# A planned S4D and SwiGLU kernel on one core: modulation columns as four tasks, the spectrum input loaded in four parts, one filling product for eight, and the plan's tasks dealt anew

## The chip, the core and the metric

The kernel runs on one core of a Trainium2 chip. The metric is the device time of one execution in microseconds (us). Engines are called as in the profile: PE is TensorE (PEld its weight loads), DVE is VectorE, ACT is ScalarE, POOL is GpSimd, SP is SyncE, which here issues nearly all DMAs. A change of the time by 0.2% (1.9 us) is about what a measurement of this kernel can tell from none.

## What is computed

```python
sa, ca, ga, sb, cb, gb = split(silu(c) @ w_mod)          # six rows of 640
h = layernorm(x) * (1 + ca) + sa                          # x: 2048 tokens x 640
K = 2 * real(sum_n C[d,n] * exp(A[d,n] * dt[d] * l))      # 640 kernels of 2048 taps, n < 128
y = irfft(rfft(h.T, 4096) * rfft(K, 4096))[:, :2048].T + h * D_skip
x = x + ga * y
h = layernorm(x) * (1 + cb) + sb
x = x + gb * ((silu(h @ w1) * (h @ w3)) @ w2)             # 640 -> 1728 -> 640
```

## The kernel before

**Two stages.** The first stage (0 to about 373 us) makes the long convolution. Channels go in five blocks of 128 (b = 0 to 4). For each block the kernel normalises the input (tasks h), makes the 128 kernels (tasks t, g), brings both into a spectrum (hh and k, then w), multiplies them and transforms back (w, z), and stores the result in DRAM (zd). The second stage (from about 382 us to the end) reads it back, adds it to x, and does the gated network as matrix products, four groups of 512 tokens: `ln2`, `ffn`, `pair_up`, `pair_down`.

**What sets the order in the first stage.** The work is cut into 1492 tasks (`Plan.add`, L177). A task names its engine or a choice of engines and the tasks it comes after. `ORDER` (L34) is the finished plan: the numbers of the tasks in the order in which `Plan.run` (L183) emits them, with a letter (a, d, p for ACT, DVE, POOL) where the engine was a choice. `InOrder` (L136) chains each engine's instructions in just that order, and semaphores do the rest. An engine whose next instruction waits does nothing else. `took`, `rank`, `take`, `give` and `port` are what the planner was told of durations, urgency and buffers; they have no effect on the chip. As every instruction of this stage is recorded through the helper at L146, most groups of the profile have that line; the tile names tell them apart.

**Modulation columns.** The second half of w_mod (sb, cb, gb) comes in five loads c0 to c4, with five products mc0 to mc4 into one PSUM tile pm (`mod_row`, L287). One task, `cols` (added at L1799, put down for ACT at 0.9 us), then calls `mod_cols` (L1247): POOL clears a corner of a tile mc, ACT copies pm into it twice, PE turns it with four products into the PSUM tile pv, and DVE writes the three columns with three small operations. All of that stands at one place of the order on each of the four engines. The last block pool (`inv`, L1125) and all products of the w tasks come after `cols`.

**A block's spectrum input.** h{b}.i.l loads a quarter of the block's x, h{b}.i.n, x and a normalise it, h{b}.i.o stores it in DRAM (hs), and h{b}.f (L1429) calls `h_fetch` (L356): four DMAs of 256 KB, one after the other, that bring the block back turned, as the tile xb. The eight products hh{b}.0 to 7 (L1448 and on) need all four.

**Behind TensorE.** A DMA that is issued while `behind` is set on SP's wrapper waits for the last PE instruction that was emitted before it (L142 to L153). `run` uses it for early loads of the second stage (fx, fw, iz: `paced`, L1145).

**The end of the first stage.** z4.3 is the last inverse product; its two halves are stored by SP, and `inverse_load` at L1208 (its DMA line is L568) reads the last block's columns for the first tokens: four DMAs from SP and four from ACT. `awake` (L1825) issues matmuls whose result nobody reads: eight (L1209), then come the inverse products (`inverse`, L1210, its lines L583 and L588), then three more (L1211), then `ln2`. The token loads of `load_x2` are held until the inverse's last product (`self.hold`), and the weights of the third tile until the reads of L1208. The first two weight tiles are loaded in the first stage and split there: fa0, fa1 (high parts, ACT), fs0, fs1 (low parts, POOL; L1173).

**Block 4 on POOL.** In the last block two of the eight spectrum products, w4.2 and w4.5, are multiplied on POOL (x0, x1, c) from a copy that ACT makes (kk); the others on DVE.

Of the kernel before, what the change touches and what calls it, by code (L numbers as in the profile page):

```python
# [10 lines left out]
F32 = mybir.dt.float32  # L11
# [7 lines left out]
P = 128  # L19
# [15 lines left out]
1 2 8 7 12 78 80 3 79 86 81 41 14 19 82 20 42 84 21 15 83 43 85 16 150p 44 17 4 22 151 18 23 28 61 45 59 30 120 31 46 121 24  # L35
10 29 25 39 153 35 26 13 62 154 60 155 47 72 74 70 76 66 89 27 48 5 93 87 91 98 49 36 100 33 95 50 94 34 51 32 88 37 52 38
152p 40 92 156d 53 96 157 90 9 158 6 54 102 159 167 104 55 170 99 11 171 168 97 56 103 183 176 172 57 105 178 173 169 58 187
184 111 177 107 185 67 192 101 122 186 68 188 174 193 160 194 189 64 179 175 123 190 180 109 161 163d 65 181 191 199 113 310
114 115 110 196 182 112 295 117 200 332 203 118 108 201 208 333a 124 300 138 305 195 116 127 204 197 128 134 130 205 206 129
135 106 140 164 202 215 63 165 218 216 217 162 166 69 209 119 211 210 125 142 126 139 132 141 219 198 207 220 133 221 131 212  # L40
225 224 213 296a 222 136 306d 226 297 227 298 307 214 223 228 71 231 416p 417 232 419 233 234 422p 420 423 247 235 144 336 143
229 308 301d 311a 236 337a 237 238 240 241 242 302 312 303 145 75 73 77 299 313 243 230 239 424 248 249 250 263 421 334 335a
251 244 252 256 257 258 253 254 259 338 245 267 339a 255 264 265 279 266 309 146 304 314 315 272 260 273 418d 147 268 246 269
148 261 340 262 270 271 342 274 283 275 282 280 281 284 276 288 290 289 341d 285 277 425 433 286 149 318 291 434 0 326 328 322
287 319a 292 437 438 327a 278 442 439 323a 440 329a 561 566 436 435 449 567d 320 293 330 444 568 343d 569 443 331d 562a 563
445 294 321a 453 441 316 317a 454 346 324 137 446 564 325d 450 678p 426 429p 451 430 452 465 347d 458 576 447 354 399 348 577d
578 459 579 679 355 455 400 456 344 349 405 365 570 565 823 828 469 345a 427 466 431 467 680p 468 460 824d 825 461 350 457 470
406 826 474 475 471 829a 366 472 580 571 572a 356 351 462 357 476 352 830 463 353 831 477 573 358 428 481 482 484 483 432 448
464 485 473 371 486 388 372 487 497 681 574 359 478 490 491 492 382 367 383 488 489 389 479 373 368 480 832 1347 575 833 827
493 374 494 369 375 501 502 1348a 498 500 499 513 495 370 376 507 1349 834a 506 835 1350 836 508 377 503 504 517 378a 380a 505  # L50
514 516 515 682 683 581 1100 594 584 582 509 595d 522 510 1101a 592 511 1102 523 1103 684p 529 530 532 685 531 583a 518 585a
519 593a 520 533 360 1351 1090 379 838 837 524 1091d 538 1092 586 525 363a 521 496 587a 361a 512 839a 534 1093 364 1094 1352
1104 384 526 385 539 840 386 590 527 596 535 591a 536 537 841 387 540 541 390 588 401 542 391 402 392 686 545 543 403 393 404
687 688 689 548 546 547 940p 695 696 697 691p 698 549 597a 550 551 589a 616 610 552 1353a 617 528 611 544 644 633 661 554 1354
555 1355 556 699 634 645 700 557 704 407 408 705 409 650 627 553 701 662 702 667 706 410 703 651 668 628 558 707 842 1085 362
843 1356 1095 381 856 844 559 858 711 690 727 692 693 715 857a 708 1086d 1096d 1087 716 845a 717 714 712 1097 1088 709 854 720
1098 855d 859a 941 718 728 713 729 730 846 852 604 847d 722 721 853d 606d 723 605a 850 848 601 719 724 560 731 732 851a 733
602a 725 734 737 849d 738 603d 736 942p 1202p 743 598 607 599a 710 735 747 608a 600d 739 744 746 745 394 694 759 943 748 395a
749 609d 612 740 753 752 613 754 741 411 614 750 755 726 751 397a 763 615 1089 1099 1357 1105 396 412a 1358a 764 414a 398 1362
413 415 760 761 775 762 756 769 768 618 757 872 619 1359 620 878 770 1360 621 629 765 766 767 771 779 873 879 780 742 781 776  # L60
778 777 946p 791 944 947 945 630 772 635 631 784 636 632 785 637 622 773 786 638 623a 774 782 625a 783 758 795 787 788 889 646
895 789 792 793 948 807 794 808 810 809 1363a 796 890 797 652 647 801 648 800 649 1364 802 790 896 798 799 811 639 1365 803
653 804 654 663 805 640a 1361 624 626 1366 641 949 1203 950 957 953p 951 954 958 955 959 1204p 960 952 655 664 642d 665 656
666 657d 812 659a 669 670 671 672 816 818 817 923 906 912 813 924 814 913 907 819 643 658 660 929 815 820 1118 860 961 930 962
821 973 967 1119d 968 862d 966 1114 1116 861a 963 806 964 822 965 977 969 978 1117a 673 676a 979 976 974 989 975 970 1115d 984
982 674d 983 971 866 867d 980 868a 863 869 981 993 865a 864d 677 675 990 992 991 1005 956 1205 870a 871a 985 994 999 998 986
1000 1120 1108 995 996 1121a 997 1109a 874 875 1110 880 987 1106 1111a 1009 972 1001 876 881 877 1002 882 1021 1006 1007 1008
891 1014 1003 1112 1010 1011 1107a 892 883 893 884 1016 1015 894 1012 1013 1025 1113a 1017 1018 908 1140 1022 1208p 1206 1023
1037 1024 1026 988 909 1031 910 1030 911 1032 885a 1027 1019 887a 1134 1151 1028 1141 1029 1135 1152 1004 1033 1041 1042 1020
1043 897 914 1034 898 915 899 916 900 917 1367 886 888 1168 1035 1174 918 1044 1169 1036 1175 1040 1038 1207 1039 1053 1047  # L70
1046 1048 1049 1045 1057 921a 1054 1055 1056 1209 1069 1210 901 1211 1212 919a 1058 1050 1062 1063 1064 925 926 1059 1060 902a
1061 922 1051 1157 1073 904a 1052 1158 931 927 1065 928 932 1066 1185 1128 1067 1070 1072 1071 1219 1220 1222 1074 933 934
1191 1078 1079 1080 920 903 905 1186 1075 1129a 1076 1130a 1081 1077 1192 1223 1125 1224 1127a 1221 1235 1374 1382 1126d 1082
1375d 1228 1229 1083 1230 935 1225 1383a 1226 1068 1084 1227 1231 1239 936a 1240 1131 1236 1238 1237 1251 1232 938d 1132d 1244
1246 1370 1122 1241 1133a 1242 1233 1245 1371d 1247 1124a 1123a 1243 1252 1255 1248 1254 1253 1213 1267 1380 1153 1376 1256
1257 1381a 1377a 1258 1159 1260 1154 1262 1155 1261 1160 1156 1249 1378 1372 1161 1263 1162 1268 1270 1215p 1216 1217 1269
1214 1136 1259 1379a 1271 1234 1250 1373a 1272 1163 1273 1264 1142 1265 1137 1276 1138 1278 1277 1139 1218 1283 1164a 1274 939
937 1165 1368 1166a 1167 1467 1275 1279 1143 1280 1187 1281 1287 1369a 1288 1472 1468 1144 1284 1285 1286 1299 1188 1145 1189
1292 1190 1293 1396 1413 1420 1193 1289 1290 1414 1397 1294 1295 1146 1421 1291 1303 1304 1266 1282 1305 1149a 1300 1302 1301
1315 1194 1308 1296 1195 1170 1309 1196 1306 1310 1171 1311 1307 1172 1312 1147a 1297 1176 1177 1316 1317 1318 1331 1197 1173  # L80
1178 1313 1179 1332 1333 1334 1150 1148 1319 1198a 1335 1298 1336 1199 1402 1180 1324 1325 1341 1340 1181d 1337 1200a 1338
1201 1403 1387 1431 1342 1320 1183a 1339 1321 1388a 1343 1344 1182 1184 1469 1473 1482 1470 1474 1345 1384 1322 1389d 1326
1327 1455 1314 1323 1346 1432 1385a 1386a 1456 1328 1329 1390 1391d 1330 1483 1471 1484 1477 1485 1466 1393 1437 1395d 1392a
1394a 1398 1404 1415 1438 1416 1399 1400 1401 1405 1406 1407 1422 1449 1408 1409a 1450 1411a 1417 1423 1424 1425 1433 1439
1434 1418 1419 1426 1412 1410 1440 1427a 1429a 1435 1436 1441 1442 1443 1487 1478 1428 1488 1430 1457 1451 1452 1444 1453 1458
1459 1460 1454 1445a 1461 1464d 1447a 1462a 1475 1446 1448 1489 1463 1465 1490 1479 1476 1480 1481 1486 1491
# [109 lines left out]
class K:  # L196
# [1673 lines left out]
```

## Time and profile before

| | |
|---|---|
| three runs | 959.39, 960.32, 961.59 us; median 960.32 |
| the profiled execution | 962.86 us, of which the span is 961.0 us |
| mean granted PE clock in it | 0.964 of full |
| busy in the span | PE 89%, PEld 71%, DVE 73%, ACT 54%, POOL 36% |
| 40 to 340 us (300 us) | PE 248.51, DVE 276.92, ACT 260.14, POOL 262.29 us busy |
| 420 to 961 us (541 us) | PE 532.70 us busy at clock 1.00, DVE 349.68, ACT 208.16, POOL 48.05 |
| DMA | 112.78 MB, mean 117 GB/s; instruction queues q8 and q14: 101 loads, 1.40 MB |

How to read it: a row of the timeline gives the start, the length, the engine, the line, the operation with its tiles, and in brackets the idle time of the engine before it with what ended that idle time; "issue" stands where nothing that the profile shows ended it. A row of the windows gives, for a stretch, the busy time of each engine (and the number of its instructions), the granted PE clock, the mean share of the 16 DMA engines, and GB/s. Most engines are over 90% busy between 40 and 340 us, so a stretch in which several of them stand still together stands out there; after 420 us it is PE alone.

### The profile page before, as it was taken

What the parts mean: (1) busy time and instruction counts of PE and PEld (TensorE: products, weight loads), DVE (VectorE), ACT (ScalarE), POOL (GpSimd) and SP (SyncE); (2) the same over time, 40 slices, a digit from 0 to 9 for tenths busy, and PEclk for the clock granted to TensorE, in tenths of its full rate; (3) what the DMA queues carried; (4) which work ended last, traced back from release to release, by engine and by line L of the source; (5) the groups of instructions that cost most, each with busy time, mean ns of one, the idle gap of its engine ahead of it and who ended that gap; (6) DMA issues with size and microseconds to landing.
All of it is one profiled execution on the core that took longest, in us unless ns stands there. A gap on an engine that the chain in (4) does not pass through costs nothing.

```text
span 961.0 us, 22047 instructions
## 1 busy us (share of the span) xinstructions
PE 856.6 (89%) x8977; PEld 679.0 (71%) x8977; DVE 701.7 (73%) x1232; ACT 521.1 (54%) x883; POOL 346.4 (36%) x358
## 2 busy tenths in 40 slices
PE   2156868988999987899999999999999999999997
PEld 1034857857778662677787778888888888888875
DVE  7898899989999944655666586466468777765753
ACT  5878999979797832532343334345234444445331
POOL 2788899989998733100000000001113222200000
PEclk9587999999999998999999999999999999999999
DMA  9955456432221457975534263232132211123242
GB/s 249 256 193 150 147 127 165 120 91 69 61 77 47 123 161 210 222 211 149 153 102 125 83 164 110 72 112 77 28 82 56 55 55 55 42 83 107 76 146 82
DMA packets 124941, 112.78 MB, mean 117 GB/s; under 512 B 12328, under 2 KB 107048, under 8 KB 123560
## 3 DMA queue, kind: packets, MB, share of 16 engines
q1 hardware_dynamic: 124072, 110.46, 42.1%
q8 instruction: 70, 1.15, 0.5%
q10 hardware_dynamic: 768, 0.92, 0.3%
q14 instruction: 31, 0.25, 0.1%
HBM read 90.38 MB, written 20.97 MB: 116 GB/s over the span
## 4 chain that ended last, share of the span: by engine, by line
PE 65%; DVE 12%; ACT 5%; issue 4%; DMA 3%; SPq 0%; DVEq 0%; ACTq 0%
PE p L813 17%; PE acc L1060 15%; PE gu L1023 7%; PE gu L1025 6%; PE gu L1024 6%; PE ps L146 5%; DVE yy L146 3%; DVE fp L146 3%; DMA wq<-in_w 2%; PE kps L146 2%; ACT tr L146 2%; PE fz L146 1%; DVE fk L146 1%; DVE xx L146 1%; PE iy L583 1%
## 5 line engine op out<-in xcount | busy, mean ns | idle before, releaser
L1023 PE MATMUL gu<-xh,wh 128*128 128x512 f32 x270 | 106.0, 398 | 1.6 <-ACT xh L602 1.4
L1025 PE MATMUL gu<-xh,wl 128*128 128x512 f32 x270 | 105.4, 390 | 0.0
L1024 PE MATMUL gu<-xl,wh 128*128 128x512 f32 x270 | 105.2, 389 | 0.0
L832 POOL TENSOR_TENSOR ws<-wp 128x256 f32<-128x256 f32 x13 | 9.6, 741 | 230.8 <-DVE x L603 116.0
L146 POOL TENSOR_TENSOR ph<-p,p 128x1024 int32<-128x1024 int32 x40 | 78.4, 1960 | 8.2 <-ACT tr L146 7.8
L146 DVE TENSOR_TENSOR yy<-yy,tr 128x512 f32<-128x512 f32 (+1 forms) x80 | 75.3, 943 | 2.8 <-ACT tr L146 2.4
L716 ACT ACTIVATE wh<-wr 128x640 fp32r<-128x640 f32 x51 | 34.9, 731 | 67.0 <-PE gu L1024 61.1
L813 PE MATMUL p<-x,wch 128*128 128x512 f32 x208 | 68.3, 389 | 0.0
L146 PE MATMUL kps<-yy,xx 128*32 128x64 f32 x2560 | 49.6, 228 | 15.6 <-DVE xx L146 11.5
L1023 PEld LDWEIGHTS gu<-xh,wh 128*128 128x128 f32 x270 | 50.6, 188 | 17.6 <-DVE al L603 2.1
L1025 PEld LDWEIGHTS gu<-xh,wl 128*128 128x128 f32 x270 | 50.7, 188 | 11.2 <-DVE wl L726 0.4
L1024 PEld LDWEIGHTS gu<-xl,wh 128*128 128x128 f32 x270 | 50.7, 188 | 10.2 <-DVE xl L603 0.2
L729 POOL MEMSET w2l<- 64x640 f32 x1 | 0.6, 632 | 156.9 <-PE acc L1060 156.9
L146 ACT ACTIVATE tr<-ph,hpi 128x512 f32<-128x512 f32 x80 | 54.6, 690 | 3.3 <-DVE xx L146 2.1
L146 DVE TENSOR_TENSOR xx<-tr,xx 128x512 f32<-128x512 f32 x80 | 54.4, 680 | 1.6 <-ACT tr L146 1.4
L146 PEld LDWEIGHTS kps<-yy,xx 128*32 128x32 f32 x2560 | 43.5, 113 | 16.9 <-POOL xs_al L146 5.2
L146 POOL TENSOR_TENSOR yy<-e,e 128x512 f32<-128x512 f32 x48 | 52.4, 1104 | 7.8 <-PE kps L146 4.1
L850 DVE TENSOR_TENSOR s<-p,s 128x512 f32<-128x512 f32 x52 | 34.7, 682 | 27.0 <-ACT s L848 23.0
L1038 DVE TENSOR_TENSOR a<-a,gu 128x512 f32<-128x512 f32 x26 | 17.8, 686 | 46.5 <-PE gu L1025 46.4
L1036 ACT ACTIVATE th<-gu 128x512 f32<-128x512 f32 x26 | 15.5, 598 | 66.4 <-PE gu L1025 66.4
L146 ACT ACTIVATE tr<-ph 128x512 f32<-128x512 int32 x80 | 47.5, 600 | 3.9 <-POOL ph L146 1.6
L146 PE MATMUL ps<-wk,xb 128*64 128x128 f32 x640 | 47.2, 296 | 2.2 <-ACT sp L146 0.9
(378 smaller groups left out, 2434.0 us busy)
## 6 DMA issues: line engine op xcount, KB each, us to landing
wr<-in_w SPq DMA_DIRECT2D x52, 320.0 KB, 3.6
zd<-zt SPq DMA_DIRECT2D x39, 256.0 KB, 3.5
w2r<-in_w SPq DMA_DIRECT2D x26, 320.0 KB, 3.0
wp<-in_w SPq DMA_DIRECT2D x26, 320.0 KB, 3.6
wq<-in_w SPq DMA_DIRECT2D x26, 320.0 KB, 3.2
low<-zd SPq DMA_DIRECT2D x48, 160.0 KB, 5.3
xs<-in_x SPq DMA_DIRECT2D x16, 320.0 KB, 10.2
hs<-hb SPq DMA_DIRECT2D x20, 256.0 KB, 2.5
```

The lines of the kernel that those rows point to most:

```text
L146: self.prev = self.k.order(f(*a, **kw), self.prev)
L583: mm = nc.tensor.matmul(py[p][c:c + 32, :n], self.wd[r:r + 64, j0 + j + p, q // 2], z[q // 2][r:r + 64, j + p, o:o + n], start=True, stop= ...
L716: self.nc.scalar.activation(wh[:, i], raw[:, i], AF.Copy)
L813: nc.tensor.matmul(to, t[:, o], y[:, k], start=start and k == i == 0, stop=stop and (k, i) == (n - 1, 2), skip_group_check=True)
L832: G.tensor_tensor(s[0], a21, a22, op=ALU.add)
L850: add = lambda o, bk, s: V.tensor_tensor(o, bk, s, op=ALU.add)
L1023: nc.tensor.matmul(pg, wh[:, k, :], xh[:, k, :], start=(k == 0), stop=False)
L1024: nc.tensor.matmul(pg, wh[:, k, :], xl[:, k, :], start=False, stop=False)
L1025: nc.tensor.matmul(pg, wl[:, k, :], xh[:, k, :], start=False, stop=(k == KT - 1))
L1036: nc.scalar.activation(th, gu[0], AF.Tanh, scale=0.5)
L1038: nc.vector.tensor_mul(a, a, gu[1])
L1060: nc.tensor.matmul(acc[k], *two(a, w), start=(m == 0 and i == 0), stop=(m == 12 and i == 2))
```

## The change

Four parts; the rest of the program stays.

1. `mod_cols` becomes four tasks: cm (clear; POOL or DVE), ca (the two copies on ACT, after cm and mc4), cp (the four products on PE, after ca), cols (the three operations on DVE, after cp). Each has its own place in the order. The new `ORDER` gives cm to DVE.
2. h{b}.f of blocks 1 to 4 becomes four tasks h{b}.fa, fb, fc, f of one DMA each, and each is issued through `paced`, so it waits for the last PE instruction emitted before it. Block 0 stays as it was.
3. `awake` before the inverse products: 1 for 8.
4. `ORDER` is a new plan of the 1507 tasks that there are now. The first 160 stay; after them most places differ, and 47 tasks go to another engine (`cols` among them; of the copies hh.e and k.e some go from DVE to ACT and about as many back).

```diff
+    def paced(self, f):
+        sync = self.nc.sync
+        sync.behind = self.nc.tensor.prev
+        f()
+        sync.behind = None
+
-    def h_fetch(self, pc):
-        for a in range(4):
+    def h_fetch(self, pc, part=slice(0, 4)):
+        for a in range(4)[part]:
             self.nc.sync.dma_start(self.xb[a * 32:(a + 1) * 32]...
...
-        self.awake(nc.tensor, po.tile([P, 512], F32, name="awake0", tag="acc4"), 8)
+        self.awake(nc.tensor, po.tile([P, 512], F32, name="awake0", tag="acc4"), 1)
...
-    def mod_cols(self, pm):
+    def cols_tasks(self, pm, prio):
...
+        add("cm", ("POOL", "DVE"), (.2, .15), clear, ["mc3"], prio, take=[("hz", 1)])
+        add("ca", "ACT", .95, keep, ["cm", "mc4"], prio, give=[("x", "mc0")])
+        add("cp", "PE", .55, turn, ["ca"], prio, take=[("f2", 1)])
+        add("cols", "DVE", .6, cols, ["cp"], prio)
...
-        add(f"h{b}.f", "SP", 0, lambda: self.h_fetch(b), [f"h{b}.{i}.o" for i in range(4)] +
-            ([f"hh{b - 1}.{i}.m" for i in range(8)] if b else ["turn1"]), W["h"](b, 4), dma=[262144] * 4)
+        old = [f"h{b}.{i}.o" for i in range(4)] + ([f"hh{b - 1}.{i}.m" for i in range(8)] if b else ["turn1"])
+        if b == 0:
+            add("h0.f", "SP", 0, lambda: self.h_fetch(0), old, W["h"](b, 4), dma=[262144] * 4)
+            return
+        for i in range(4):
+            add(f"h{b}.f" + ("abc"[i] if i < 3 else ""), "SP", 0, lambda i=i: self.paced(lambda: self.h_fetch(b, slice(i, i + 1))),
+                [f"h{b}.f" + "abc"[i - 1]] if i else old, W["h"](b, 4), dma=[262144], port="behind")
...
-        add("cols", "ACT", .9, lambda: self.mod_cols(pm[1]), ["mc4"], W["col"], take=[("f2", 1), ("hz", 1)], give=[("x", "mc0")])
-        add("colsf", None, 0, None, ["cols"], give=[("f2", "cols"), ("hz", "cols")])
+        self.cols_tasks(pm, W["col"])
+        add("colsf", None, 0, None, ["cols"], give=[("f2", "cp"), ("hz", "cm")])
```

The numbers of `ORDER`, turned into names at the places that the prediction speaks of:

```
PE around the columns      before: k0.3.m g0.4.p mc4 (cols) g0.5.p      after: g0.4.p mc4 k0.3.m cp g0.5.p
SP before them             before: c3 h0.0.o h0.2.o c4 h0.1.o h0.3.o h0.f   after: c3 c4 h0.2.o h0.1.o h0.3.o h0.0.o h0.f
SP, block 2                before: h2.3.o h3.0.l z0.0.o0 h2.f h4.1.o    after: h2.3.o h3.2.l h2.fa h2.fb h2.fc h3.0.l z0.0.o1 h2.f
the parts of block 2 wait  after: fa for hh1.3.m; fb, fc and f for g1.6.p
SP, block 3                after: h3.fa h4.2.o z1.0.o0 z1.0.o1 h3.fb h4.3.o z1.1.o0 h3.fc z1.1.o1 h3.f
PE, last block             before: w4.0.k w4.1.k w4.2.k w4.3.k w4.6.f z4.0.z w4.4.k w4.5.k z4.1.z w4.7.k w4.6.k z4.2.z z4.3.z
                           after:  w4.6.f w4.2.k w4.0.k w4.1.k w4.4.f w4.3.k z4.0.z w4.5.k w4.4.k z4.1.z w4.6.k w4.7.k z4.2.z z4.3.z
POOL, last block           before: w4.2.x0 x1 c, w4.5.x0 x1 c, fs0 fs1   after: w4.2.x0 fs0 w4.2.x1 c, w4.5.x0 x1 c, fs1
```

More of the change, by code (lines that the diff above doesn't have):

```diff
@@ L39 @@
[L39 to L50, printed above, removed]
@@ L83 @@
[L83 to L86, printed above, removed]
+1 2 8 7 12 78 80 3 79 86 81 41 14 19 82 20 42 84 21 15 83 43 85 16 153p 44 17 4 22 154 18 23 28 61 45 59 30 120 31 46 121 24
@@ new lines @@
+10 29 25 39 156 35 26 13 62 157 60 158 47 72 74 70 76 66 89 27 48 5 93 87 91 98 49 36 100 33 95 50 94 34 51 32 88 37 52 38
+155p 40 92 159d 53 96 160 90 9 161 6 54 102 162 170 104 55 173 99 11 174 171 97 56 103 186 179 175 57 105 181 176 172 58 190
+187 111 180 107 188 67 195 101 122 189 68 191 177 196 163 197 192 64 182 178 123 193 183 109 164 166d 65 184 194 202 113 313
+114 115 110 199 185 112 298 117 203 335 206 118 204 124 303 138 308 140 167 198 211 116 212 108 106 168 205 165 142 127 207
@@ L87 @@
+1492 1498 1357 1405 1470 1335 1358 1340 1341 1407d 1406d 1471 1404d 1342 1408 1464 1409d 1481 1410a 1430 1431 1490 1465 1486
+1499 1413 1419 1446 1437 1414 1432 1415 1420 1416 1421 1422 1438 1493 1500 1423 1447 1424a 1439 1440 1454 1448 1425 1449 1455
+1426a 1427 1502 1450 1451 1491 1433 1434 1456 1457 1458 1441 1466 1467 1444d 1442a 1472 1443 1445 1503 1459 1473 1474 1468
+1475 1469 1476 1462a 1463 1479a 1477a 1460d 1461 1504 1478 1480 1505 1494 1495 1496 1501 1506
 """
@@ L1245, in run, with clear, keep, turn @@
         close("ps", "po", "pair", "mid", "keep", "xc", "wp", "xp", "wrp")
-    def mod_cols(self, pm):
-        nc = self.nc
-        m = self.ring("mc")
-        nc.gpsimd.memset(m[96:, 384:], 0.0)
-        nc.scalar.activation(m[:, :384], pm[:, :384], AF.Copy)
-        nc.scalar.activation(m[:96, 384:], pm[:96, 384:], AF.Copy)
-        pv = self.psg.tile([P, 512], F32, name="pv", tag="f", bufs=3)
-        for o in range(4):
-            nc.tensor.matmul(pv[:, o:16:4], m[:, o * P:(o + 1) * P], self.ident[:, 0:P:32], start=True, stop=True)
-        for a, (add, mul) in enumerate(((0.0, 1.0), (1.0, 1.0), (0.0, 0.5))):
-            nc.vector.tensor_scalar(self.cols[:, a, :], pv[:, a * KT:(a + 1) * KT], add, mul, op0=ALU.add, op1=ALU.mult)
+    def cols_tasks(self, pm, prio):
+        nc, add = self.nc, self.plan.add
+        x = {}
+        def clear(e):
+            x["m"] = m = self.ring("mc")
+            self.eng(e).memset(m[96:, 384:], 0.0)
+        def keep():
+            m = x["m"]
+            nc.scalar.activation(m[:, :384], pm[1][:, :384], AF.Copy)
+            nc.scalar.activation(m[:96, 384:], pm[1][:96, 384:], AF.Copy)
+        def turn():
+            m, pv = x["m"], self.psg.tile([P, 512], F32, name="pv", tag="f", bufs=3)
+            x["pv"] = pv
+            for o in range(4):
+                nc.tensor.matmul(pv[:, o:16:4], m[:, o * P:(o + 1) * P], self.ident[:, 0:P:32], start=True, stop=True)
+        def cols():
+            for a, (plus, mul) in enumerate(((0.0, 1.0), (1.0, 1.0), (0.0, 0.5))):
+                nc.vector.tensor_scalar(self.cols[:, a, :], x["pv"][:, a * KT:(a + 1) * KT], plus, mul, op0=ALU.add, op1=ALU.mult)
+        add("cm", ("POOL", "DVE"), (.2, .15), clear, ["mc3"], prio, take=[("hz", 1)])
+        add("ca", "ACT", .95, keep, ["cm", "mc4"], prio, give=[("x", "mc0")])
+        add("cp", "PE", .55, turn, ["ca"], prio, take=[("f2", 1)])
+        add("cols", "DVE", .6, cols, ["cp"], prio)
     def h_norm(self, pc, b, out, e):
```

80 lines of the change are left out of this document (44 added, 36 removed).

## The prediction, made before the result was known

> **What bounds the kernel now.** I read the page first, then the windows over the first stage, then the timeline of the stretches that stand out, then the chain of waits at the end of the stage.
>
> ```profile
> span 961.0 us, 22047 instructions
> 60.00:80.00 20.00, 10.98 (x193) 6.94 (x195) 19.00 (x39) 16.47 (x30) 16.75 (x19) 0.74 0.39 132
> 80.00:100.00 20.00, 14.64 (x236) 10.94 (x232) 15.36 (x25) 15.12 (x28) 16.78 (x16) 0.67 0.77 220
> 100.00:120.00 20.00, 17.56 (x425) 16.16 (x424) 18.45 (x32) 18.23 (x31) 17.28 (x19) 0.99 0.35 111
> 160.00:180.00 20.00, 18.08 (x414) 16.74 (x418) 19.82 (x37) 19.19 (x36) 19.18 (x18) 1.00 0.59 149
> 180.00:200.00 20.00, 16.34 (x475) 13.31 (x465) 16.16 (x26) 15.04 (x24) 15.55 (x15) 0.91 0.40 94
> 200.00:220.00 20.00, 17.09 (x407) 13.08 (x408) 18.86 (x33) 18.70 (x35) 18.92 (x20) 1.00 0.40 108
> 240.00:260.00 20.00, 18.70 (x566) 16.40 (x566) 17.66 (x29) 15.82 (x27) 17.72 (x20) 1.00 0.11 30
> 280.00:300.00 20.00, 18.55 (x596) 15.71 (x598) 17.62 (x28) 17.95 (x33) 16.92 (x14) 1.00 0.18 49
> ```
>
> The columns are the stretch, then PE, PEld, DVE, ACT and POOL busy, the granted clock, the DMA share and GB/s. In the first stage DVE is the fullest engine, near 19 or 20 of 20 us, with ACT and POOL close behind; no single faster operation helps much. Two stretches fall out: at 80 to 100 and 180 to 200 us DVE is idle for 4.64 and 3.84 us, and ACT and POOL with it. An idle time that all share moves the end of the stage. The change touches both places, and the end of the stage.
>
> **Part 1, the columns.** The timeline of 84 to 101 us:
>
> ```profile
> 87.55 1.02 PE L146 MATMUL pm<-xs_w,sc 128*32 128x512 f32 x6
> 91.58 0.64 ACT L146 ACTIVATE mc<-pm 128x384 f32<-128x384 f32 x2
> 92.11 0.83 PE L146 MATMUL pv<-ident,mc 128*128 128x4 f32 x6 [3.54 <-ACT mc L146]
> 93.54 0.20 POOL L146 MEMSET mc<- 32x128 f32 x1
> 93.79 0.59 PE L146 MATMUL pv<-ident,mc 128*128 128x4 f32 x2 [0.85 <-POOL mc L146]
> 94.42 0.30 DVE L146 TENSOR_SCALAR cols<-pv 128x5 f32<-128x5 f32 x3 [1.86 <-PE pv L146]
> 96.47 0.39 ACT L146 ACTIVATE ks<-kps 128x256 f32<-128x256 f32 x1 [4.26 <-PE kps L146]
> 97.47 1.22 DVE L146 TENSOR_TENSOR yy<-yy,tr 128x1024 f32<-128x1024 f32 x1 [2.15 <-ACT tr L146]
> ```
>
> mc4's products end at 88.57. PE's next work is pv, but ACT reaches the copies only at 91.58, and POOL the memset only at 93.54, each behind other work of its own queue. PE stands 3.54 + 0.85 us; the products queued behind pv are late, so ACT stands 4.26 us, and DVE 1.86 + 2.15 = 4.01 us. In the new order the clearing is done before, a product task (k0.3.m) lies between mc4 and cp and covers the copies, and the columns' DVE work stands after it. What goes is DVE's idle time above that of the neighbours: 4.64 - (1.00 + 1.55)/2 = 3.4 us. Bounds: nothing, if c4 or ACT is late again, and 4.0, the two waits of DVE. The memset moves onto DVE; no row shows it there, POOL's took 0.20, so I charge 0.2 on the fullest engine, between 0 and 0.4. Part 1: **3.2 us**. What is late next is h0.f's landing and the 2 MB load wb; the windows' DMA share of 0.77 shows room, so I add nothing.
>
> **Part 2, the fetch.** The timeline and the windows of single microseconds around 190 us:
>
> ```profile
> 187.87 1.75 SPq L146 DMA_DIRECT2D xb<-hs  x4
> 195.01 1.95 PE L146 MATMUL ps<-wk,ks 64*64 64x64 f32 x83 [3.59 <-issue]
> ```
> ```profile
> 190.00:191.00 1.00, 1.00 (x56) 0.84 (x49) 1.00 (x3) 1.00 (x3) 0.83 (x2) 1.00 1.09 209
> 193.00:194.00 1.00, 0.00 (x0) 0.00 (x0) 0.00 (x0) 0.00 (x0) 0.59 (x1) 1.00 0.64 113
> 196.00:197.00 1.00, 1.00 (x35) 0.88 (x28) 1.00 (x2) 1.00 (x4) 0.00 (x0) 0.50 0.09 16
> ```
>
> PE stops in the middle of a run of like products, waits 3.59 us for nothing that the profile names, and goes on a little over 1 us after the 1 MB fetch has drained (the DMA share is 1.09 at 190 and 0.64 in 193 to 194). Nothing else is missing, so I read it as PE's own code, which has to be loaded too, standing behind the burst; that is an inference, the profile does not say it. Afterwards the clock is 0.50. The stretch loses 3.84 - (0.18 + 1.14)/2 = 3.2 us of DVE against its neighbours. In parts of 256 KB the wait can be a quarter; but in block 2, fb, fc and f wait for the same product and leave together, three quarters of the burst. I keep a quarter of the loss back: **2.4 us**, bounds 0 and 3.6. [...]
>
> The price of part 2 is 12 more waits of SP on PE (16 parts in place of four issues). Behind each stand h loads and z stores in SP's queue; they have three zt buffers in hand and, in the new order, come from tasks emitted later, so I take 0; the other end is a rival below.
>
> **Part 3, one filling product.** The end of the stage: the reads of the last block's columns (view of the tile low), the timeline, and windows:
>
> ```profile
> L568 SPq DMA_DIRECT2D low<-zd x4: 574/590/637, 369.9 to 372.9; - x4
> DMA to landing us min/median/max: 2.2/2.8/3.2
> ```
> ```profile
> 373.04 8.96 PE L146 MATMUL awake<-x_low,ident 128*128 128x512 f32 x16
> 381.93 0.66 PE L583 MATMUL iy<-low,x_low 64*32 64x128 f32 x24
> 383.37 2.84 PE L146 MATMUL awake<-x_low,ident 128*128 128x512 f32 x6
> 387.52 0.16 DVE L250 SCALAR_TENSOR_TENSOR rs_n_n<-mv_n,rs_y_n 128x4 f32<-128x4 f32 x1
> 388.75 2.40 PE L634 MATMUL tp<-ident,xn 128*128 128x128 f32 x20 [2.54 <-ACT xn L618]
> ```
> ```profile
> 374.00:376.00 2.00, 2.00 (x4) 0.91 (x3) 1.17 (x7) 0.00 (x0) 0.61 (x1) 0.50 0.25 56
> 376.00:378.00 2.00, 2.00 (x5) 0.77 (x5) 0.00 (x0) 0.00 (x0) 0.00 (x0) 0.81 0.99 283
> ```
>
> The last read is issued at 372.9 and lands 2.2 to 3.2 us later, so by about 376.0. The inverse product starts at 381.93, held by the sixteen filling instructions alone. With two of them it can start at 376.0: 5.9 us earlier. The clock is then still at half (it rose some 3.7 us after 373.04: a mean of 0.81 over 376 to 378 is half for 0.76 us). The inverse's 32 short products and the first filling products after them take longer: the 24 take 0.66 at full clock, so about 0.7 more at half; with the small ones after it I take 0.9. The chain behind it (DVE's statistics to 387.52, ACT, the transposes) is DVE's and ACT's and keeps its length. Part 3: **5.0 us**; bounds 3.1 (the clock falls behind, a rival below) and 5.9.
>
> Is DMA late next? The token loads move up too, but the weights are in front of them. The row that decides is the fifth weight tile:
>
> ```profile
> 416.76 1.68 DVE L726 TENSOR_TENSOR wl<-wr,wh 128x640 fp32r<-128x640 f32 x2 [5.15 <-ACT wh L716]
> 428.87 0.19 PEld L1023 LDWEIGHTS gu<-xh,wh 128*128 128x128 f32 x1 [0.52 <-issue]
> ```
>
> Its split is ready at 418.44 and PE begins on it at 428.87: 10.4 us in hand, more than the 5.0 that PE gains. So DMA costs nothing.
>
> **Part 4, the new deal.** The amount of work stays; about as many copies go to ACT as come back. The trace cannot show the new order. I take 0. Bounds: DVE's idle time in 240 to 260 and 280 to 300 is 2.34 and 2.38 us, about 1.7 above a well filled stretch; two such holes more or two fewer give 3.4 either way. One place I looked at closely: POOL now does fs0 inside w4.2.
>
> ```profile
> 358.87 1.99 PE L146 MATMUL fz<-fp,wz 64*128 64x512 f32 x8 [0.32 <-POOL fp L146]
> 365.80 3.05 POOL L146 TENSOR_TENSOR wl<-wr,wh 128x640 fp32r<-128x640 f32 x2 [6.30 <-ACT wh L146]
> 368.81 1.53 POOL L146 TENSOR_TENSOR w2l<-w2r,w2h 128x640 fp32r<-128x640 f32 x1
> ```
>
> These 4.6 us stand between w4.2's first and second operation; PE already waits 0.32 us for POOL at z4.2. The plan pays by putting w4.2.k before w4.0.k and w4.1.k. I take 0, at worst 2.5.
>
> **The sum.** 3.2 + 2.4 + 5.0 + 0 = 10.6 us. The profiled execution took 962.86 (span 961.0 and 1.86 around it), so it would take 952.3; it stands 2.5 us above the median of the three runs, 960.32, and from that the forecast is **949.7 us**.
>
> **The rivals.**
>
> *The clock stays down* (951.6). With one filling product PE works from 376.0, but in short products with waits between; if that doesn't raise the clock, the transposes and the first up products run at half until it does. The first 3.7 us of filling products went at half, so half of that, 1.9, is lost: 949.7 + 1.9. Against it: three filling products after the inverse remain (2.84 us at full clock, twice that at half), and PE's idle time before the transposes, 2.54 us now, stays near 2. [...]
>
> *The burst was not the cause* (952.1). If PE's stop at 191 us has another cause, or the code load meets the three parts that leave together, part 2 gives nothing: 949.7 + 2.4. For it: the profile names no releaser. Against it: the stop ends with the burst.
>
> *The deal gives it back* (about 960). The order was dealt anew as a whole; six holes of 1.7 us like the one at 240 would take 10.2 of the 10.6 us. For it: nearly every place after the 160th changed, and such holes are there now with no cause that a part of the change removes.
>
> *SP's queue stands behind PE* (963.6). Each of the parts waits for PE's last emitted product, and the stores and loads behind it wait too. A product task that they wait for takes 1.16 us:
>
> ```profile
> 189.18 1.16 PE L146 MATMUL kps<-yy,xx 128*32 128x64 f32 x64
> ```
>
> If each of the 12 added waits puts that on the path of a z store or an x load whose buffer is needed, 13.9 us come on top: 949.7 + 13.9. It decides from 0.9 us per wait (10.6/12). For it: block 3 puts six stores between its parts. Against it: three zt buffers and loads issued a block ahead.
>
> *The deal closes holes as well* (946.3): two holes of 1.7 fewer, 949.7 - 3.4.
>
> **How the numbers follow.** Forecast 0.44 (its own range 946.3 to 953.1, the bounds of the new deal), clock 0.13, burst 0.13, a better deal 0.06: these four are faster, 0.76 together. Given back: 0.11. SP's queue: 0.13. Faster means below 958.4, slower above 962.2. The range starts at 944.0 (part 1 at 4.0, part 2 at 3.6, part 3 at 5.9, and 2.8 of the better deal) and ends at 960.5, behind the case in which the gain is given back; outside are the slower case and a few in a hundred below.
>
> **What would show it.** Right: no wait of PE for mc, and DVE over 18 of 20 us around it; no "issue" gap over 1.5 us near the parts; two filling instructions before the L583 products, these within 1 us of the last landing, and the transposes about 5 us closer to the reads of L568; from there to the end the same length as now. Wrong: a new gap in which DVE, ACT and POOL are idle together; SP waiting on PE ahead of a z store that ACT's zt copies wait for; a granted clock of 0.5 at the transposes; or a second stage that is longer from the transposes to the end.

## The result and the profile after

The changed kernel takes 946.0 us (five runs, 945.76 to 949.13) against 959.56 us for the kernel before in the same rounds (958.97 to 961.59): a ratio of 0.9863, 95% interval 0.984 to 0.9887. That is 13.1 us less of 959.6, between 10.8 and 15.4. The forecast was 949.7 us, its range 944.0 to 960.5. The profiled execution took 946.81 us.

The page, and then the windows of the first stage, with the columns as before:

```profile
span 945.0 us, 22045 instructions
```
```profile
60.00:80.00 20.00, 11.40 (x202) 6.40 (x203) 15.08 (x33) 17.69 (x33) 19.68 (x21) 0.76 0.58 205
80.00:100.00 20.00, 17.46 (x432) 14.77 (x432) 19.23 (x34) 19.10 (x35) 19.90 (x17) 0.92 0.72 193
180.00:200.00 20.00, 19.77 (x604) 15.96 (x594) 18.96 (x31) 17.73 (x33) 18.42 (x20) 1.00 0.28 76
240.00:260.00 20.00, 19.87 (x506) 17.03 (x506) 20.00 (x36) 17.75 (x34) 19.44 (x22) 1.00 0.15 42
280.00:300.00 20.00, 19.12 (x460) 16.89 (x460) 19.56 (x35) 17.16 (x31) 18.69 (x18) 1.00 0.18 50
```

The two stretches that fell out have closed: DVE 19.23 us where it had 15.36 (80 to 100), 18.96 where it had 16.16 (180 to 200). But so have the smaller holes with which no part of the change was concerned: 20.00 for 17.66, 19.56 for 17.62. A new hole stands at 60 to 80 (15.08 for 19.00), ahead of the columns; the six other traces of the new order have 17.17 to 19.02 there, so it belongs to this execution.

The columns, in the timeline:

```profile
88.35 0.17 DVE L147 MEMSET mc<- 32x128 f32 x1
88.80 0.63 ACT L147 ACTIVATE mc<-pm 128x384 f32<-128x384 f32 x2
89.32 1.06 PE L147 MATMUL pv<-ident,mc 128*128 128x4 f32 x8 [0.29 <-ACT mc L147]
90.88 0.29 DVE L147 TENSOR_SCALAR cols<-pv 128x5 f32<-128x5 f32 x3
```

PE's 3.54 + 0.85 us of waiting have become 0.29, and DVE's operations start without a wait. Then the end of the first stage:

```profile
357.02 3.30 SPq L575 DMA_DIRECT2D low<-zd  x4
359.36 1.89 PE L147 MATMUL awake<-x_low,ident 128*128 128x512 f32 x2
361.18 2.08 PE L590 MATMUL iy<-low,x_low 64*32 64x128 f32 x32
363.19 2.84 PE L147 MATMUL awake<-x_low,ident 128*128 128x512 f32 x6
368.59 3.38 PE L641 MATMUL tp<-ident,xn 128*128 128x128 f32 x20 [2.56 <-ACT xn L625]
```

From the first read to the transposes it is 368.59 - 357.02 = 11.57 us; before it was 388.75 - 369.85 = 18.90. So 7.3 us are gained here, but the transposes take 3.38 us for 2.40. The windows show why, and a second loss stands 30 us later in the timeline:

```profile
368.00:370.00 2.00, 1.41 (x12) 1.41 (x13) 0.77 (x2) 1.35 (x2) 0.00 (x0) 0.96 1.31 345
370.00:372.00 2.00, 1.97 (x10) 1.57 (x8) 1.62 (x2) 1.19 (x2) 0.00 (x0) 0.50 0.96 186
372.00:374.00 2.00, 1.07 (x3) 0.88 (x4) 0.98 (x2) 2.00 (x5) 0.46 (x1) 0.50 0.98 220
374.00:376.00 2.00, 2.00 (x6) 1.60 (x5) 2.00 (x3) 1.86 (x3) 2.00 (x2) 0.50 1.08 241
376.00:378.00 2.00, 2.00 (x9) 1.56 (x8) 1.06 (x1) 0.49 (x1) 0.51 (x1) 0.83 1.02 220
```
```profile
402.06 1.54 ACT L723 ACTIVATE wh<-wr 128x640 fp32r<-128x640 f32 x2 [9.80 <-DMA wr<-in_w]
402.83 1.63 DVE L733 TENSOR_TENSOR wl<-wr,wh 128x640 fp32r<-128x640 f32 x2 [9.13 <-ACT wh L723]
404.98 0.48 DVE L595 TENSOR_TENSOR x<-iy,x 128x320 f32<-128x320 f32 x1
405.52 0.50 PE L1030 MATMUL gu<-xh,wh 128*128 128x512 f32 x1 [1.99 <-DVE x L595]
```

The granted clock is 0.50 for some 6.8 us across the transposes. And a wait is handed on: the fifth tile's weights (wr) land late, ACT waits 9.80 us to round them (wh), DVE 9.13 us for ACT to form the low part (wl), and behind wl in DVE's queue stands the addition of an inverse product to x (L595), which frees a PSUM bank; PE waits 1.99 us for that bank, not for the weights. The second stage, which the change leaves as it was but for the filling, gives back part of what its start gained.

### The profile page after: what moved, and what is told of

Its sections match the earlier page's. It is cut to its first block, busy times and chain, and to the rows that moved or that the text cites. A ratio compares the mean times of both kernels' runs of the same rounds, so it can differ in the third digit from the quotient of the medians.

```text
span 945.0 us, 22045 instructions
## 1 busy us (share of the span) xinstructions
PE 850.9 (90%) x8963; PEld 676.5 (72%) x8963; DVE 698.3 (74%) x1232; ACT 521.6 (55%) x886; POOL 346.4 (37%) x355
## 3 DMA queue, kind: packets, MB, share of 16 engines
q1 hardware_dynamic: 124072, 110.46, 42.8%
## 4 chain that ended last, share of the span: by engine, by line
PE 67%; DVE 11%; DMA 10%; POOL 4%; ACT 3%; issue 3%; SPq 1%; DVEq 0%; ACTq 0%; POOLq 0%
PE p L820 17%; PE acc L1067 17%; PE gu L1030 6%; PE gu L1032 6%; PE gu L1031 6%; PE ps L147 4%; DMA low<-zd 2%; DVE yy L147 2%; PE kps L147 2%; PE fz L147 2%; PE fk L147 2%; DVE fp L147 2%; PE fh L147 2%; POOL yy L147 2%; DMA xs<-in_x 1%
## 5 line engine op out<-in xcount | busy, mean ns | idle before, releaser
L147 PE MATMUL fh<-sp,wb 128*64 128x128 f32 x640 | 45.5, 288 | 3.8 <-DVE fp L147 2.2
```

Source lines behind the costliest of these rows:

```text
L147: self.prev = self.k.order(f(*a, **kw), self.prev)
```

## The experiments

Each kernel below ran beside the kernel before on its chip. The kernel before scatters there from 953.9 to 965.0 us from one execution to the next, and a profile shows one execution only; so ratios carry the verdicts, and rows of a trace carry places. Ratios are also given as us of 959.6.

| kernel | median, us | ratio (95%) | us against before |
|---|---|---|---|
| before, columns as four tasks | 957.13 | 0.9986 (0.9965 to 1.0008) | -1.3 |
| before, block 3's fetch in parts | 957.52 | 0.9986 (0.9963 to 1.0008) | -1.3 |
| before, one filling product | 954.52 | 0.9956 (0.9933 to 0.9978) | -4.2 |
| the new deal alone | 954.29 | 0.9928 (0.9906 to 0.9951) | -6.9 |
| before, without block 2's fetch | 958.88 | 0.9983 (0.9965 to 1.0) | -1.6 |
| before, without block 3's fetch | 956.67 | 0.9975 (0.9956 to 0.9994) | -2.4 |
| before, a long product in the short run | 959.08 | 1.0005 (0.9987 to 1.0022) | +0.5 |
| after, columns at one place | 951.32 | 0.9903 (0.988 to 0.9926) | -9.3 |
| after, fetch whole | 948.13 | 0.9901 (0.9869 to 0.9934) | -9.5 |
| after, eight filling products | 949.15 | 0.9908 (0.9884 to 0.9932) | -8.8 |
| after, tokens later | 944.11 | 0.9821 (0.9796 to 0.9845) | -17.2 |
| after, tokens later, fetch whole | 944.88 | 0.9853 (0.9828 to 0.9879) | -14.1 |

The four parts alone make 1.3 + 1.3 + 4.2 + 6.9 = 13.7 us, the whole change 13.1; but part 2 was tried alone in one block only, and each of the four is uncertain by about 2 us. Undone one at a time, the first three come to 3.8 + 3.6 + 4.3 = 11.7 us, which leaves less for the deal than the 6.9; with about 3 us of uncertainty on each, these rounds don't say whether the parts simply add. The split is what the forecast had otherwise. My theory after the two traces was that its three parts hold with other sizes and that DMA and the clock take back some of part 3; the rival was that the new deal makes much of the gain by itself.

### The columns

Alone, in the old order (cm ahead on DVE, ca behind mc4, cp behind g0.5.p); the lines of `ORDER` are given here and below by the names of the tasks:

```diff
- ... h0.f g0.6.m0 ... mc4 g0.6.s1 g0.4.r g0.6.s2 cols g0.5.p ...
+ ... h0.f cm g0.6.m0 ... mc4 ca g0.6.s1 g0.4.r g0.6.s2 g0.5.p cp cols ...
```

> The kernel before with the columns alone as four tasks, put into the old order by hand: the clearing on VectorE ahead of g0.6.m0, ScalarE's copies right behind mc4, TensorE's four products behind g0.5.p, VectorE's three operations behind them. The forecast priced part 1 at 3.2 us: 959.6 - 3.2 = 956.4 us, with no wait of TensorE for the tile mc over 1 us. The progress of the product groups, which are 6 us ahead behind this place: 953.6 us if all of that is the columns'. The rival that the new deal makes that gain and the columns alone only move the wait: 959.6 us.

And undone in the new order:

```diff
- ... k0.1.e cm g0.5.m3 ... h0.f ca cp g0.5.m4 g0.6.m0 cols g0.6.s1 g0.4.r g0.6.s2 ...
+ ... k0.1.e g0.5.m3 ... h0.f g0.5.m4 g0.6.m0 g0.6.s1 g0.4.r g0.6.s2 cm ca cp cols ...
```

> The changed kernel with the four tasks of the columns put back to one place of its order, behind g0.6.s2 and ahead of g0.5.p as before, the clearing on POOL: part 1 undone, the rest kept. The forecast: 946.0 + 3.2 = 949.2 us, with TensorE standing at the columns' products as in the kernel before (3.5 and 0.9 us). By the product group behind the columns in the run with the columns alone (4.4 us earlier): 950.4 us. The rival that the next waits give the gain back, as the timed rounds of the columns alone would have it (1.3 us): 947.3 us.

The same window of both, the columns alone first, then undone, and there PE's row of the timeline:

```profile
80.00:100.00 20.00, 14.74 (x338) 11.40 (x332) 18.48 (x31) 18.13 (x33) 19.40 (x17) 0.89 0.78 216
```
```profile
80.00:100.00 20.00, 15.02 (x372) 12.51 (x362) 16.72 (x27) 16.45 (x29) 17.01 (x15) 0.86 0.75 211
```
```profile
91.09 0.83 PE L147 MATMUL pv<-ident,mc 128*128 128x4 f32 x6 [2.68 <-ACT mc L147]
```

Where they stand, the columns are worth 18.48 - 15.36 = 3.1 us of DVE's time in the old order and 19.23 - 16.72 = 2.5 in the new, close to the 3.2 of the forecast; undone, PE's wait for mc is back at 2.68 us. Timed, they are worth 1.3 us alone (between a gain of 3.4 and a loss of 0.8) and 13.1 - 9.3 = 3.8 undone, with about 3 us either way (5.3 by the medians). The trace with the columns alone is of an execution of 953.20 us, 3.9 below that kernel's median, so it shows them at their best. The place agrees with the forecast; how much later waits give back isn't settled by these rounds.

### The fetch and PE's stop

The whole fetch in the new order, and the same with the later token loads of the last section:

```diff
-  lambda i=i: self.paced(lambda: self.h_fetch(b, slice(i, i + 1)))
+  (lambda: self.h_fetch(b)) if i == 0 else None
```

> The changed kernel with the four DMAs of a block's fetch issued together again, in blocks 1 to 4, at the place of the first part and without waiting for TensorE; the order of all else is kept: part 2 undone. The forecast priced part 2 at 2.4 us: 948.4 us, with one stop of TensorE of 2 us or more for which the profile names no releaser, next to a fetch. The rival that the burst is not the cause: 946.0 us and no such stop beyond those of the changed kernel. The rival from the progress of the product groups, which gain 5 us in that stretch: 951 us.

> The changed kernel with the later token loads, and with a block's four fetch DMAs issued together again, without waiting for TensorE: part 2 undone where the start of the second stage no longer scatters. Forecast: 944.1 + 2.4 = 946.5 us. The theory that the new order took the fetch away from the run of short products and the parts add nothing: 944.1 us, with no stop next to a fetch above those of the run with the later loads. By the timed rounds without the later loads (0.9901 against 0.9863): 947.7 us, in a few executions only.

The first took 945.7 to 946.0 us in three runs and 950.3 to 953.8 in three; the second 942.8 to 946.0 against 941.2 to 945.1. Neither profile has a stop without a releaser next to a fetch, and none above 1.61 us, where the changed kernel has one of 2.30. The profile of the first is of a run of 945.95 us, though; what made the other three 4 to 8 us longer, no trace shows. So in the new order the parts are worth 3.6 us by the one pair of ratios and 3.1 by the other, each with an uncertainty as large, and 0.8 us by the medians of the second pair. In the traces, the 3.59 us stop of the old order had gone without them. What made it, then? Three kernels in the old order ask that; the first two leave PE's instructions as they are.

```diff
-  add(f"h{b}.f", "SP", 0, lambda: self.h_fetch(b), ...
+  add(f"h{b}.f", "SP", 0, None if b == 2 else lambda: self.h_fetch(b), ...   # then: if b == 3
```

> The kernel before without block 2's fetch of 1 MB; its products read block 1's data, so the output is another, and TensorE's instructions are the same. The forecast's reading, the burst holds up TensorE's code: the stop near 191 us, 3.59, 2.69 and 1.37 us in three traces of the old order and always at the same product, falls below 0.5 us, 956.0 to 957.2 us. The rival that the burst is not the cause: a stop of 1.4 to 3.6 us at the same product, 959.6 us. A third: the run of short products outpaces its own code loads and the burst only adds to it: a stop of about 1.4 us, 957.4 to 958.5 us.

> The kernel before without block 3's fetch, the one that is issued at 187.87 us next to TensorE's stop; its products read block 2's data, so the output is another, and TensorE's instructions are the same. The run without block 2's fetch had left out the wrong one: that one goes out at 164.31 us. The forecast's reading, the burst holds up TensorE's code: the stop, 1.37 to 3.59 us in four traces of the old order, falls below 0.5 us and the median by 1.4 to 3.2 us, to 956.4 to 958.2 of 959.6 us. The rival that the run of short products outpaces its code loads without any burst: the stop stays between 1.4 and 3.6 us, 959.6 us.

The first was aimed wrongly. The fetch at 187.87 is block 3's; block 2's goes out at 164.31. With block 2's left out the stop stayed:

```profile
193.25 2.33 PE L146 MATMUL ps<-wk,ks 64*64 64x64 f32 x82 [1.65 <-issue]
```

With block 3's left out the same 128 products run without one:

```profile
190.16 1.16 PE L146 MATMUL kps<-yy,xx 128*32 128x64 f32 x64
191.24 2.63 PE L146 MATMUL ps<-wk,ks 64*64 64x64 f32 x128
193.80 2.07 PE L146 MATMUL fz<-fp,wz 64*128 64x512 f32 x8
```

The queue view shows what was late. In the kernel before q1 carries data (110.46 MB) and q8 instructions, 70 packets of 16 KB; as its page counts 8977 matmuls and as many weight loads, 256 for each packet, I take q8 for PE's code. From 186.9 to 192.1 us of the kernel before, and then from 192.1 to 196:

```profile
q1 hardware_dynamic: 468, 0.78, 63.9%
xb<-hs SPq DMA_DIRECT2D x4, 256.0 KB, 5.4
...
q1 hardware_dynamic: 179, 0.30, 40.9%
q8 instruction: 1, 0.02, 2.1%
```

And the same stretches without block 3's fetch, moved by the 1.0 us by which this execution is later: 187.9 to 193.1, and 193.1 to 197.

```profile
q1 hardware_dynamic: 50, 0.02, 2.1%
q8 instruction: 1, 0.02, 1.1%
...
q8 instruction: 1, 0.02, 1.5%
```

Beside the burst no instruction packet starts for over 5 us; the next one starts at 192.13, 2.95 us after the kps products of 189.18, and without the burst 0.02 us before those of 190.16. By then PE has been through a run of short products (64 of them in 1.16 us), and it stands from 191.43 until 195.01, 1.54 us past the end of that packet at 193.47. This holds throughout: between 100 and 940 us the fourteen traces have 35 stops of PE over 1 us without a releaser, and each ends 1.23 to 1.68 us after the end of a q8 packet (1.38 to 1.61 in the four of the kernel before). So I read such a stop as PE waiting for its code. When the code was asked for, the traces don't show, nor how the burst delays it.

The changed kernel's stop of 2.30 us, which ends at 327.71, is of the same kind: it breaks a run of short products (kps), and no q8 packet starts between 319.67 and 325.04 us, while q1 takes 84.6% of the DMA engines' time (319.7 to 325.0). All seven traces of the new order have it, with 1.60 to 2.73 us; no run here tries to remove it.

Does the short run matter too? One task of eight long products was moved into it, with ACT's copies of the result, and the burst kept:

```diff
- ... k1.1.e0 g2.1.p ... k1.0.m k1.3.m ... z0.2.z ... z0.2.v0 ... z0.2.v1
+ ... k1.1.e0 z0.2.z z0.2.v0 z0.2.v1 g2.1.p ... k1.0.m k1.3.m ...
```

> The kernel before with one product task (z0.2.z, eight products of 512 columns) and ScalarE's two copies of it moved ahead of g2.1.p, into the run of short products in which TensorE stops; the fetch at 188 us is kept. The theory that the run of short products outpaces its own code loads: 2 us of long products in it give the loads time, the stop falls by 2 us, below 1 us, and the median by 1 to 2.5 us, to 957.1 to 958.6 of 959.6 us. The forecast's reading, the burst alone: the stop stays at 1.4 to 3.6 us, wherever the code ends, and the time at 959.6 us.

```profile
186.71 1.74 SPq L146 DMA_DIRECT2D xb<-hs  x4
189.00 2.34 PE L146 MATMUL fz<-fp,wz 64*128 64x512 f32 x8 [1.24 <-ACT sp L146]
192.44 2.10 PE L146 MATMUL ps<-wk,ks 64*64 64x64 f32 x128
196.26 1.13 PE L146 MATMUL fk<-sp,wb 128*64 128x128 f32 x16 [1.73 <-ACT sp L146]
```

The stop is gone with the burst in place: by these traces this stop takes both, a burst and a run of short products. The time did not move, as 1.24 + 1.73 us of waits for ACT came in. Last, part 2 by itself, in block 3 and the old order:

```diff
-  h3.f at its place
+  h3.fa at its place, h3.fb, h3.fc, h3.f behind w1.1.k, g2.3.p, w2.0.f, each through paced
```

> The kernel before with part 2 alone and in block 3 alone, in the old order: block 3's fetch as four tasks, the first at the old place, the others behind the next three product tasks, each waiting for TensorE's last product emitted. The forecast: the stop goes (below 0.5 us), and with it 2.4 us: 957.2 of 959.6 us; without that fetch at all the ratio was 0.9975, also 957.2 us. The rival that SP's queue stands behind TensorE: the stores of z0.2 and z0.3 are queued behind the first part, ScalarE waits for a zt buffer, 959.6 us or more. The rival that the stop moves to the run of short products next to the parts: 959.6 us, with a stop over 1 us between 200 and 215 us.

```profile
191.19 1.50 PE L146 MATMUL ps<-wk,ks 64*64 64x64 f32 x83 [0.28 <-issue]
198.81 0.31 SPq L146 DMA_DIRECT2D xb<-hs  x1
204.54 1.66 SPq L146 DMA_DIRECT2D xb<-hs  x3
```

The stop falls to 0.28 us because the wait for PE moves the fetch from 187.87 to 198.81, out of the short run; three parts leave together there, at 204.54, and PE has no stop over 1 us without a releaser before 242.29. Whether smaller parts would help at the old place, no run shows. The timed gain is 1.3 us, within a gain of 3.6 and a loss of 0.8.

### The new deal

Columns at one place, fetch whole, eight filling products (the edits above together), in the new order:

> The new order with parts 1, 2 and 3 all undone (columns at one place, a block's fetch issued whole, eight filling products): the new deal alone. The forecast took the deal at 0: 959.6 us. What the undone parts leave of the 13.1 us (3.2 to 4.3 for the filling, up to 3.6 for the fetch, 1.3 to 4.4 for the columns) is 1 to 5 us: 954.6 to 958.6 us. The rival that the deal makes most of the gain of the first stage by itself: 951 to 953 us.

6.9 us, between 4.7 and 9.0: the rival. One row of the windows over 220 us for the kernel before, the deal alone and the whole change:

```profile
100.00:320.00 220.00, 194.23 (x4757) 162.28 (x4758) 206.71 (x350) 195.70 (x344) 199.03 (x196) 0.98 0.37 97
```
```profile
100.00:320.00 220.00, 200.50 (x4865) 165.68 (x4866) 213.39 (x363) 201.44 (x354) 204.34 (x198) 0.98 0.38 96
```
```profile
100.00:320.00 220.00, 201.60 (x4904) 165.76 (x4904) 215.12 (x365) 203.38 (x356) 203.75 (x198) 0.98 0.38 102
```

DVE is idle for 220 - 206.71 = 13.3 us before, 6.6 with the deal alone, 4.9 with all. One trace is a rough measure of this: the kernel before with one filling product, which differs from the kernel before only behind this stretch, has 210.29 busy, so 9.7 idle, and the old order with the columns alone 7.3. Hole by hole: with the deal alone DVE is busy 18.24 us from 180 to 200 (16.16 before), as the last of block 2's spectrum products come later in the new order (the last begin at 195.06 us in the kernel with the whole fetch, at 185.24 before) and block 3's fetch goes out behind them, at 200 us there. From 280 to 300 it is busy 18.82 us (17.62 before, 17.60 to 17.98 in five more traces of the old order, but 19.02 with the columns alone). From 240 to 260 it is 18.77 (17.66 before), but that is no proof, as the old order with one filling product has 18.77 as well. Only the hole at the columns stays, 15.85 from 80 to 100 (15.36). Which of the moved tasks closes which hole was not tried.

### The filling products

Alone in the kernel before, and undone in the changed one:

```diff
-        self.awake(..., name="awake0", tag="acc4"), 8)
+        self.awake(..., name="awake0", tag="acc4"), 1)
```

> The kernel before with one filling product in place of eight, and nothing else: part 3 alone. The forecast: 959.6 - 5.0 = 954.6 us. The theory from the two traces (7.9 us at the inverse's start, 2.0 lost to the clock, 2.4 to the wait behind VectorE's copy of the third weight tile): 956.1 us, with the granted clock at 0.50 at the transposes and a wait of TensorE of about 2 us some 35 us after them. The rival that DMA bounds the second stage: 959 to 959.6 us.

> The changed kernel with eight filling products ahead of the last inverse in place of one: part 3 undone, everything else kept. The forecast priced part 3 at 5.0 us: 946.0 + 5.0 = 951.0 us. The theory from the two traces: the inverse starts 7.9 us earlier after its reads, but 2.0 us go to a granted clock of 0.50 at the transposes and 2.4 us to a wait of TensorE behind VectorE's copy of the third weight tile, so 3.5 us are left: 949.5 us, with the clock back at 1.00 at the transposes and the wait near 405 us gone. The rival that DMA bounds the second stage anyway: 946.0 to 947.0 us.

4.2 us alone, and 13.1 - 8.8 = 4.3 undone (3.1 by the medians). From the first read to the transposes it is 378.08 - 366.11 = 11.97 us with one filling product in the old order and 374.33 - 356.79 = 17.54 with eight in the new, against 18.90 and 11.57: a gain of 6.0 to 6.9. The wait behind wl takes 2.70 us of it with one product in the old order:

```profile
410.09 1.52 ACT L716 ACTIVATE wh<-wr 128x640 fp32r<-128x640 f32 x2 [9.21 <-DMA wr<-in_w]
413.52 0.50 PE L1023 MATMUL gu<-xh,wh 128*128 128x512 f32 x1 [2.70 <-DVE x L588]
```

With eight there is none. The clock is another matter. With eight filling products in the new order the windows show it at half as well (the third number from the end is the clock):

```profile
373.00:375.00 2.00, 0.67 (x6) 0.67 (x7) 1.37 (x4) 1.64 (x2) 0.00 (x0) 1.00 1.11 271
375.00:377.00 2.00, 2.00 (x13) 2.00 (x12) 0.63 (x1) 0.30 (x2) 0.00 (x0) 0.56 1.04 241
377.00:379.00 2.00, 1.04 (x6) 0.64 (x4) 1.01 (x3) 1.92 (x4) 0.00 (x0) 0.59 0.92 195
```

Over the fourteen traces it falls near the transposes in five of eight with eight products and in five of six with one, so the filling is not what decides it; the last section shows what goes with it.

### Tokens later

If the weights come late behind the token loads, those can wait: the third group's until the fourth tile's inverse product, the fourth group's until the eighth's.

```diff
-            if b == 0 and m in (2, 4):
-                self.load_x2(m // 2 + 1)
+            if b == 0 and m in (4, 8):
+                self.load_x2(m // 4 + 1, self.last)      # held until this product
```

> The changed kernel with the token loads of the third and fourth group taken out of the start of the second stage: each waits for an inverse product of the network's fourth or eighth tile. The theory that the fifth tile's weights come late behind 2.6 MB of tokens, and that VectorE, waiting to copy them, holds up the sum that frees TensorE's bank: TensorE's wait near 404 us goes, 946.0 - 2.3 = 943.7 us. The rival, that the columns' reads alone keep the DMA engines full until then: 946.0 us, with ScalarE's wait for the weights still over 8 us. Another, that SP now stands behind TensorE with the next weights: over 947 us.

```profile
385.75 9.27 SPq L706 DMA_DIRECT2D wr<-in_w  x6
```
```profile
391.54 0.72 ACT L723 ACTIVATE wh<-wr 128x640 fp32r<-128x640 f32 x1
392.04 1.55 DVE L733 TENSOR_TENSOR wl<-wr,wh 128x640 fp32r<-128x640 f32 x2
395.56 0.48 DVE L595 TENSOR_TENSOR x<-iy,x 128x320 f32<-128x320 f32 x1
```

The weights go out at 385.75 us in place of 396.98, nobody waits for them, and PE's wait for x is gone. At 944.11 us (941.23 to 945.14, ratio 0.9821) this is the fastest kernel here, 1.9 us below the changed one, whose runs in other rounds all lie above it (945.76 to 949.13); the two intervals of the ratio overlap a little.

## Why the prediction was right, and where it was not

The forecast was 3.7 us above the result; its rival that the deal closes holes as well stood at 946.3. Step by step:

- **Part 1, 3.2 us.** Right in mechanism and place: 3.1 and 2.5 us of DVE's time in the window, PE's wait for mc 0.29. Timed, 1.3 and 3.8, both uncertain.
- **Part 2, 2.4 us.** The reading held as far as the traces go: the stop ends 1.54 us behind the end of a q8 packet that starts late beside the burst, and leaving that fetch out removes the stop, and 2.4 us (0.6 to 4.2). The step that failed is "in parts of 256 KB the wait can be a quarter", reckoned with the parts of block 2. The fetch at 187.87 was block 3's; what removed the stop was the fetch's other place, the size was not tried at the old one, and the deal had moved that fetch already. So the gain was credited to the wrong part: 1.3 us alone, and 0.8 to 3.6 in the new order, for which no trace shows a cause. The stop's length was also taken from one execution: three other traces of the old order that keep burst and run have 2.69, 1.65 and 1.37 us, so 3.59 was the longest seen.
- **Part 3, 5.0 us.** Reads to transposes gained 7.3 us, more than the bound of 5.9: the step "by about 376.0", 6.1 us behind the first read, was mis-sized; the products started 361.18 - 357.02 = 4.16 us behind it, with no wait for a DMA. What failed is "So DMA costs nothing". The 10.4 us in hand were counted for PE's use of the fifth tile; the first to wait for it are ACT's wh and DVE's wl, and behind wl, in the same queue, stands the addition that frees a bank. That cost PE 1.99 us here, and 0.69, 2.70 and 3.26 in the three other traces with one filling product and the token loads at their old place. Net 4.2 us.
- **The clock stays down, 1.9 us.** The clock was at 0.50 across the transposes for 6.8 us, but it does so with eight products too. Its reason, that one product can't raise it, isn't borne out: the clock rose at 363.01 us, 3.65 us behind the first filling product, and fell again at 369.84, behind the gap ahead of the transposes.
- **Part 4, the deal, 0.** Wrong: 6.9 us (4.7 to 9.0), beyond the bound of 3.4. The bound counted two holes of 1.7 us; DVE's idle time from 100 to 320 us was 13.3 us in this trace (9.7 in another with the same tasks) and could have been read from one row. A new order can close any of it. DVE is the engine to read here: from 40 to 340 us it alone was over 90% busy (276.92 of 300 us), the others 83 to 87%.
- **SP behind PE, 963.6.** It did not come. ACT waits for a zt buffer once, ahead of 345.20 us, long after the last part has gone out (271.02); in the kernel before it waits once too.
- **fs0 on POOL, at worst 2.5.** From 330 to 357 us PE waits nowhere for POOL, and its weight loads 1.0 us in all, in three places.

That the sum came near is in part luck, as errors offset: the deal was 6.9 too low, part 2 about 1, part 3 about 0.8 and part 1 up to 1.9 too high.

## What to carry to other kernels

When an order is dealt anew, bound what it can give by the idle time of the fullest engine over the whole stage, in more than one execution, not by a pair of holes; and ask of each hole whether the deal closes it before crediting another part with it. A buffer "in hand" is counted to the first instruction that waits for it, on any in-order queue, and then to what stands behind that instruction. Where an engine stops with no releaser in a run of short instructions, look whether the queue of instruction loads is silent beside a large DMA and the stop ends shortly behind its next packet (1.2 to 1.7 us here); if so, move the DMA out of the run.

## What the runs showed of the hardware

Unexpected was how regular the clock's falls are. Worked out from the windows (each 2 us, the missing share of the clock times 4), the time at half speed near the transposes is 0 in four traces, 3.40 to 3.44 us in eight and 6.80 to 6.84 in two, the same length whatever the kernel, once or twice. PE's idle time ahead of the transposes says nothing on it: 2.54 us in the kernel before without a fall, 2.56 in the changed kernel with one.

The traces also show what tells like gaps apart. Between two steps of the clock lie 3.41 us or a whole multiple of that (6.83 us at full from 363.01 and 6.83 at half from 369.84 in the changed kernel), so the time around the transposes can be cut into stretches of 3.41 us at these steps. In all ten traces with a fall, PE was busy for 0.8 to 1.4 us in the stretch just ahead of it: 1.25 us in the changed kernel, from 366.42 to 369.84, where 2.2 us of the gap of 2.56 lie in one stretch. In the four without a fall no stretch from the filling products to the first up products has less than 1.6 us: in the kernel before, the cut at 386.99 leaves 0.78 us of the gap of 2.54 ahead of it and 1.76 behind, and the stretch behind it has 1.65 us of work. The gap is 2.52 to 2.76 us in thirteen of the fourteen traces (1.72 in the other, without a fall), so among these what went with a fall is where the gap lay against the steps; no run here moves it on purpose. One fall further from the transposes doesn't fit: the changed kernel's at 359.60 us came behind a stretch with 1.94 us of work.
